# Attention with wider products, masks on GpSimd and another order of the work

## The chip, the cores and the metric

The kernel runs on one core of one Trainium2 chip. The metric is the device time of one execution in microseconds (us); less is better. Some runs are also recorded by the hardware profiler, and all stretches below are us from the start of such a record.

## The reference

Three parts follow each other. Attention runs over 4 batches x 8 heads of 576 rows and 64 columns:

```python
scores = scale * np.matmul(q, k.transpose(0, 1, 3, 2))
scores = np.where(causal, -1000000000.0, scores)
scores = scores - scores.max(-1, keepdims=True)
a = np.exp(scores)
a /= a.sum(-1, keepdims=True) + 1e-09
local = np.matmul(a, v)
...
mem_out = mem_ret / mem_norm
g = 1.0 / (1.0 + np.exp(-beta))[None, :, None, None]
return (g * mem_out + (1 - g) * local).astype(np.float32)
```

`mem_ret` and `mem_norm` are products of phi(q) with a matrix and a vector per head. The 2304 rows of the result then go to 8 experts (each row to one, at most 288 rows to each, chosen by a greedy pass over sorted gate logits), through two layers of the expert, and through a last block `max(x @ w1, x @ w2, x @ w3) @ w_out`.

## The kernel before

Everything is float32, most of it split into a high and a low part that are multiplied separately. The work of attention is a list of tasks in 16 pairs of heads; pair p has keys around 10 p. `Plan.run` (L143) sets the order: it always takes the task that can start first by the costs written beside the tasks (us x 1000), and the lower key among equals. Each engine then executes its own tasks in that order. `PRIO` (L59) holds the offsets of the keys.

For one pair:

- SyncE's queue loads K (`Kr`), Q (`Qr`), Q again for the memory part (`QN`), V, V transposed (`VT`) and the memory matrix (`MZ`) (L316 to L333). ScalarE casts high parts (`KX`, `QX`, `KB`), VectorE subtracts low parts (L353, L358).
- Scores (`piece`, L386): TensorE makes Q x K in blocks of the PSUM tile `s`, each begun by a mask product (`mask_s`, L394, 128 columns), and VectorE takes row maxima from it (`nm`, L413). TensorE turns the maxima (L440), ScalarE copies them (`nmt`) and its own DMA queue writes them as a row of the low part of Q (`QL`, L449 and L450).
- Transposed scores (`score`, `tprod`, L549): the tile `t` holds K x Q less the maxima, from a product with `KX` (L557) and one with `KB` and `QL` (L558). Diagonal blocks begin with a mask product (`mask_t`, L556): five blocks per head, four of 128 columns and one of 64. There are three groups of 512 columns per head and a small one for both. ScalarE takes the exponential into `PT` (L575, L577).
- Output products (`fAV`, L585): for row block j (0 to 4), blocks kb up to j of `PT` are the weights, and 73 columns of V (64 of V, 8 of the expert gate, one of ones) stream. A float32 product is two instructions, so a pair has 60. VectorE divides by the sums and adds the memory part (`norm`, L610). There is one PSUM tile `av` for all pairs.
- Gate products (`g0`, L460): V transposed times 16 columns of the gate matrix `WB`, ten instructions; ScalarE copies them into V (L466). Memory products (`mem`, L509): phi times `MZ`, 146 columns, in two parts. The 16 gate columns of `MZ` are copied by GpSimd (L489) from `MG`, which four groups of small products make at the start from the matrix `mT` (in the tile `m2raw`, L685 to L703).

`fill` (L673) is 48 matmuls of zeros that the first output products wait for; they run where TensorE has nothing else in the start. Between the pairs 24 loads and conversions of the last block's weights are spread (`conv`, L723). Routing and experts follow as a second plan. `ML` (L1074) is the low part of those weights, in 12 tiles.

Of the kernel before, what the change touches and what calls it, by code (L numbers as in the profile page):

```python
# [17 lines left out]
try:  # L18
# [22 lines left out]
FILL = 48  # L41
# [17 lines left out]
PRIO = {"load": -14, "prep": -12, "cb": 3, "S": -11, "N": -11, "nmte": "ACT", "G": -4, "phi": -6, "mem": (-2, -1), "memx": "ACT", "T": 0, "E": 0, "A": 4,  # L59
        "norm": 4, "gate": -9, "m2": (4.0, 6.3, 6.0)}  # L60
# [6 lines left out]
def rows(j):  # L67
    return 128 if j < 4 else 64
# [159 lines left out]
def attention(g, tc, ctx, consts, beta, qT, kT, qN, v1, vT, mz, mT, wg, xd, L, m2):  # L228
# [15 lines left out]
    mt = cs.tile([128, 128], BF, name="mask_t")  # L244
# [4 lines left out]
    G.affine_select(mt, zero[:, :128], pattern=[[1, 128]], compare_op=OP.is_ge, fill=MASK, base=0, channel_multiplier=-1)  # L249
# [13 lines left out]
    WB = cs.tile([128, H // 2, 2, E], F32, name="wb")  # L263
# [4 lines left out]
    def ldw(e):  # L268
        for i in range(2):
            nc.sync.dma_start(WB[64 * i:64 * i + 64, :, i], wg.rearrange("(c i d) e -> i d c e", i=2, d=64)[i])  # L270

# [35 lines left out]
    def pair(p):  # L307
# [30 lines left out]
        for u, (a, z) in enumerate(parts):  # L338
# [35 lines left out]
            tcb.append(add(k + W["cb"], {"ACT": act(w)}, cb, [tK[u], tkb[p] if p < len(KB) else None],  # L374
                           use=U_("Kr") + ([] if not u else U_("KB")), **N_("KB")))
            tsq.append(add(k + W["cb"] + .01, {"DVE": dve(w)}, sq, [tcq[u]], use=U_("Qr", "QX") + ([] if not u else U_("QL")), **N_("QL")))
# [9 lines left out]
        def piece(key, prods, reds):  # L386
# [18 lines left out]
            cost = sum(mm(z - a) * (1 if j < 4 else 2) + 60 * diag for j, i, a, z, c, diag in prods)  # L405
# [13 lines left out]
        for i in range(2):  # L419
            piece(ks + .1 * i, [(3, i, 0, 512, 0, True)], [(0, 512, 1, 4 * i + 3, 0)])  # L420
        for i in range(2):
            piece(ks + .2 + .1 * i, [(2, i, 0, 384, 0, True)], [(0, 384, 1, 4 * i + 2, 0)])
        if p == 0:
            for i in range(2):
                piece(ks + .4 + .1 * i, [(1, i, 0, 256, 0, True), (0, i, 0, 128, 256, True)], [(0, 256, 1, 4 * i + 1, 0), (256, 128, 1, 4 * i, 0)])
            piece(ks + .6, [(4, 2, 512, 576, 0, True)], [(0, 64, 1, 9, 0)])
        else:
            for i in range(2):
                piece(ks + .4 + .1 * i, [(1, i, 0, 256, 0, True), (0, i, 0, 128, 256, True)] + [(4, 2, 512, 576, 384, True)] * i,
                      [(0, 256, 1, 4 * i + 1, 0), (256, 128, 1, 4 * i, 0)] + [(384, 64, 1, 9, 0)] * i)  # L430
        piece(ks + .7, [(4, 2, 0, 512, 0, False)], [(0, 512, 1, 8, 0)])
# [28 lines left out]
        def g0(e):  # L460
            for j in range(NJ):
                PE.matmul(MEM[:rows(j), 4 * C + 16 * j:4 * C + 16 * j + 16], r.VT[:, 128 * j:128 * j + rows(j)],  # L462
                          WB[:, pp].rearrange("p i e -> p (i e)"), start=True, stop=True)

# [84 lines left out]
        def tprod(o, i, gr, c):  # L549
            for kb, a, z in gr:  # L550
# [3 lines left out]
                diag = a == 128 * kb  # L554
                if diag:
                    PE.matmul(o[:kr, c:c + kr], identb[:kr, :kr], mt[:kr, :kr], start=True, stop=False, skip_group_check=True)  # L556
                PE.matmul(d, r.KX[:, i, ks_], r.QX[:, i, a:z], start=not diag, stop=False, skip_group_check=True)  # L557
                PE.matmul(d, r.KB[:, i, ks_], r.QL[:, i, a:z], start=False, stop=True, skip_group_check=True)  # L558
                c += z - a

        def score(key, items, out):
# [9 lines left out]
            def fE(e):  # L571
                if not hasattr(r, "PT"):
                    r.PT = tile("PT", [128, 2, 1600])
                if len(items) > 1:
                    A.activation(r.PT[:64, :, 1536:], o.t[:64, :128].rearrange("p (i q) -> p i q", i=2), AF.Exp, scale=0.125)  # L575
# [18 lines left out]
        outs = []  # L594
# [12 lines left out]
        kq = n + 3 + W["norm"]  # L607
# [80 lines left out]
    for b in range(B):  # L688
        bm = Buf(R["mem"])

        def f0(e, b=b):
            for c in range(4):
                m = mt_.t[:, (4 * b + c) * 64:(4 * b + c) * 64 + 64]
                for i in range(2):
                    PE.matmul(MEM[64 * i:64 * i + 64, 8 * c:8 * c + 8], m, WB[:, c, i], start=True, stop=True)

# [5 lines left out]
        t = add(-10.5, {"PE": 600}, f0, [tl, twb], new=[bm], use=[bt])  # L702
        tmg.append(add(-10.4, {"ACT": 156}, f1, [t], use=[bm]))  # L703
# [739 lines left out]
```

## Time and profile before

| | |
|---|---|
| median of 3 runs | 933.59 us (929.9 to 953.56) |
| the profiled execution | 935.49 us |
| its span, first to last instruction | 933.8 us |
| mean granted TensorE clock | 0.935 of full speed |
| TensorE busy | 889.8 us, 95% of the span |
| VectorE, ScalarE, GpSimd busy | 572.9, 365.2 and 80.0 us |

A row of the profile names the line, the engine, the operation, and the tiles as out<-in. PE is TensorE, DVE is VectorE, ACT is ScalarE, POOL is GpSimd, SPq and ACTq are the DMA queues that SyncE and ScalarE issue. The clock that was granted to TensorE is given as a share of full speed. Matmuls overlap, so from one start to the next is what a product costs, and the length of one is longer than that.

### The profile page before, as it was taken

What the parts mean: (1) busy time and instruction counts of PE and PEld (TensorE: products, weight loads), DVE (VectorE), ACT (ScalarE), POOL (GpSimd) and SP (SyncE); (2) the same over time, 40 slices, a digit from 0 to 9 for tenths busy, and PEclk for the clock granted to TensorE, in tenths of its full rate; (3) what the DMA queues carried; (4) which work ended last, traced back from release to release, by engine and by line L of the source; (5) the groups of instructions that cost most, each with busy time, mean ns of one, the idle gap of its engine ahead of it and who ended that gap; (6) DMA issues with size and microseconds to landing.
All of it is one profiled execution on the core that took longest, in us unless ns stands there. A gap on an engine that the chain in (4) does not pass through costs nothing.

```text
span 933.8 us, 17447 instructions
## 1 busy us (share of the span) xinstructions
PE 889.8 (95%) x6880; PEld 811.5 (87%) x6880; DVE 572.9 (61%) x1481; ACT 365.2 (39%) x826; POOL 80.0 (9%) x145
## 2 busy tenths in 40 slices
PE   7999999999999937989999999999999999999997
PEld 5788888888888827889999999999899999999996
DVE  5456876767567489897577478377277463343421
ACT  3546566566645531322331341331331332432311
POOL 1000000000100005520200200200200201000001
PEclk8578999989889957979999999999999999999999
DMA  7546755465451116142440440530540441230100
GB/s 181 147 113 173 198 166 169 142 185 154 134 194 49 47 61 152 46 90 96 94 136 1 95 135 2 112 118 1 90 151 2 98 131 27 100 104 1 46 1 34
DMA packets 38529, 92.82 MB, mean 99 GB/s; under 512 B 10096, under 2 KB 12272, under 8 KB 38448
## 3 DMA queue, kind: packets, MB, share of 16 engines
q1 hardware_dynamic: 35152, 82.20, 29.3%
q0 software_dynamic: 2976, 9.44, 6.2%
q8 instruction: 54, 0.88, 0.4%
q14 instruction: 27, 0.22, 0.1%
q10 hardware_dynamic: 320, 0.07, 0.0%
HBM read 82.18 MB, written 9.45 MB: 98 GB/s over the span
## 4 chain that ended last, share of the span: by engine, by line
PE 76%; issue 14%; DVE 4%; POOL 1%; DMA 1%; ACT 1%; ACTq 1%; SPq 1%; POOLq 0%; DVEq 0%
PE av L591 12%; PE w L1187 9%; PE w L1189 9%; PE w L1188 9%; PE acc L1188 4%; PE acc L1187 4%; PE acc L1189 4%; PE t L557 4%; PE mem L509 3%; PE t L558 3%; PE s L396 3%; PE rps L935 2%; PE mem L462 1%; PE t L556 1%; PE s L400 1%
## 5 line engine op out<-in xcount | busy, mean ns | idle before, releaser
L1187 PE MATMUL w<-yh,mh 128*128 128x288 f32 x576 | 174.3, 303 | 0.0
L1189 PE MATMUL w<-yh,ml 128*128 128x288 f32 x576 | 170.3, 296 | 0.0
L1188 PE MATMUL w<-yl,mh 128*128 128x288 f32 x576 | 170.1, 295 | 0.0
L591 PE MATMUL av<-V,PT 128*128 128x73 f32 (+2 forms) x960 | 128.4, 286 | 1.6 <-ACT PT L575 0.7
L591 PEld LDWEIGHTS av<-V,PT 128*128 128x128 f32 (+2 forms) x960 | 116.1, 194 | 9.0 <-ACT PT L575 1.5
L1187 PEld LDWEIGHTS w<-yh,mh 128*128 128x128 f32 x576 | 109.2, 190 | 3.0
L1188 PEld LDWEIGHTS w<-yl,mh 128*128 128x128 f32 x576 | 109.0, 189 | 2.9
L1189 PEld LDWEIGHTS w<-yh,ml 128*128 128x128 f32 x576 | 109.0, 189 | 0.0
L1158 DVE TENSOR_TENSOR wlo<-wraw,whi 128x1024 fp32r<-128x1024 f32 x64 | 80.1, 1253 | 41.5 <-ACT whi L1154 41.4
L1292 DVE TENSOR_TENSOR mt<-w,mt 128x288 f32<-128x288 f32 x96 | 43.6, 454 | 80.2 <-PE w L1189 78.0
L577 ACT ACTIVATE PT<-t 128x512 f32<-128x512 f32 x96 | 56.6, 609 | 87.0 <-PE t L558 85.8
L1154 ACT CAST whi<-wraw 128x1024 fp32r<-128x1024 f32 x64 | 66.8, 1049 | 40.3 <-PE acc L1188 22.2
L1188 PE MATMUL acc<-hl,whi 128*128 128x288 f32 x256 | 77.2, 302 | 3.2 <-DVE hl L1095 2.7
L1187 PE MATMUL acc<-hh,whi 128*128 128x288 f32 x256 | 77.0, 301 | 1.0 <-ACT hh L1089 1.0
L413 DVE TENSOR_REDUCE nm<-s 128x1 fp32r<-128x512 f32 (+4 forms) x160 | 69.1, 471 | 13.9 <-PE s L396 11.7
L1189 PE MATMUL w<-xhi,wlo 128*128 128x288 f32 x256 | 76.4, 298 | 1.1 <-DVE wlo L1158 1.1
L1187 PE MATMUL w<-xhi,whi 128*128 128x288 f32 x256 | 76.9, 300 | 0.0
L1188 PE MATMUL w<-xlo,whi 128*128 128x288 f32 x256 | 76.4, 298 | 0.0
L1189 PE MATMUL acc<-hh,wlo 128*128 128x288 f32 x256 | 76.0, 297 | 0.0
L1054 ACT CAST gc<-mt 128x32 fp32r<-128x32 f32 (+2 forms) x72 | 17.5, 243 | 143.4 <-DVE mt L1292 143.4
L557 PE MATMUL t<-QX,KX 128*128 128x512 f32 (+2 forms) x192 | 70.0, 366 | 0.0
L1095 DVE SCALAR_TENSOR_TENSOR hl<-w,hh 128x288 fp32r<-128x288 f32 x64 | 29.0, 455 | 63.3 <-ACT hh L1089 61.3
(222 smaller groups left out, 1821.4 us busy)
## 6 DMA issues: line engine op xcount, KB each, us to landing
wraw<-in_wr SPq DMA_DIRECT2D x64, 512.0 KB
Qr<-in_qT SPq DMA_DIRECT2D x30, 288.0 KB
m2raw<-in_m2w SPq DMA_DIRECT2D x12, 512.0 KB
V<-in_v SPq DMA_DIRECT2D x16, 365.0 KB
QN<-in_qN SPq DMA_DIRECT2D x16, 288.0 KB
VT<-in_vT SPq DMA_DIRECT2D x16, 288.0 KB
Kr<-in_kT SPq DMA_DIRECT2D x15, 288.0 KB
xd<-x SPq DMA_DIRECT2D x16, 256.0 KB
```

The source lines that it names most:

```text
L396: PE.matmul(d, r.QX[:, i, 128 * j:128 * j + 128], r.KX[:, i, a:z], start=False, stop=True, skip_group_check=True)
L413: V.tensor_reduce(r.nm[:, col:col + k], o.s[:, c:c + k * w].rearrange("p (k w) -> p k w", k=k), axis=AX.X, op=OP.max)
L557: PE.matmul(d, r.KX[:, i, ks_], r.QX[:, i, a:z], start=not diag, stop=False, skip_group_check=True)
L577: A.activation(r.PT[:, items[0][0], out:out + 512], o.t, AF.Exp, scale=0.125)
L591: PE.matmul(av[:m, i, j], r.PT[:kr, i, o:o + m], V4()[:kr, kb, i], start=kb == 0, stop=kb == j)
L1095: V.scalar_tensor_tensor(lo(), src(), 0.0, hi().bitcast(F32), op0=OP.max, op1=OP.subtract)
L1154: A.copy(x.W[fb][0], x.RAW[fb])
L1158: V.tensor_sub(x.W[fb][1], x.RAW[fb], x.W[fb][0].bitcast(F32))
L1187: nc.tensor.matmul(o, wh, rh, start=start, stop=False)
L1188: nc.tensor.matmul(o, wh, rl, start=False, stop=False)
L1189: nc.tensor.matmul(o, wl, rh, start=False, stop=stop)
L1292: V.tensor_max(q.mt, o.pt[:, :T], q.mt)
```

## The change

The mask product of the transposed scores goes, and with it the tile `mask_t`; GpSimd sets the masked part of `PT` to zero behind the exponential instead (`select`: two diagonal blocks of a head at once, and the two 64-column blocks together, five per pair). Output products of row blocks 0 to 3 stream 112 columns of V instead of 73, and gate products 112 columns of a gate matrix that is now held three times side by side. The extra columns land in the columns of the next row block, which is written after. The keys change: within a pair, score groups, output blocks and maxima are spread over ten steps, head 1 five steps after head 0; loads are due ten steps earlier; the small products of `mT` get keys 1 to 12; the output tasks' costs are raised. `fill` has 78 matmuls. `ML[0]` gets a tile of its own.

```diff
-FILL = 48
+FILL = 78
...
-PRIO = {"load": -14, "prep": -12, "cb": 3, "S": -11, "N": -11, "nmte": "ACT", "G": -4, "phi": -6, "mem": (-2, -1), "memx": "ACT", "T": 0, "E": 0, "A": 4,
-        "norm": 4, "gate": -9, "m2": (4.0, 6.3, 6.0)}
+PRIO = {"load": -24, "prep": -18, "cb": 8, "S": -14, "ds": 1.2, "N": -5, "nmte": "ACT", "G": -3, "phi": -6, "mem": (1.6, 6.6), "memx": "ACT",
+        "T": (0.5, 2.2, 3.5), "A": 5, "norm": 14, "gate": 6, "m2": (0.0, 6.3, 8.0), "tmg": (1, 6, 9, 12)}
+VW, GW = 112, 112
...
-    G.affine_select(mt, zero[:, :128], pattern=[[1, 128]], compare_op=OP.is_ge, fill=MASK, base=0, channel_multiplier=-1)
...
-    WB = cs.tile([128, H // 2, 2, E], F32, name="wb")
+    WB = cs.tile([128, 3, H // 2, 2, E], F32, name="wb")
...
     def ldw(e):
-        for i in range(2):
-            nc.sync.dma_start(WB[64 * i:64 * i + 64, :, i], wg.rearrange("(c i d) e -> i d c e", i=2, d=64)[i])
+        for a in range(3):
+            for i in range(2):
+                nc.sync.dma_start(WB[64 * i:64 * i + 64, a, :, i], wg.rearrange("(c i d) e -> i d c e", i=2, d=64)[i])
...
         def g0(e):
             for j in range(NJ):
-                PE.matmul(MEM[:rows(j), 4 * C + 16 * j:4 * C + 16 * j + 16], r.VT[:, 128 * j:128 * j + rows(j)],
-                          WB[:, pp].rearrange("p i e -> p (i e)"), start=True, stop=True)
+                w = GW if j < 4 else 16
+                PE.matmul(MEM[:rows(j), 4 * C + 16 * j:4 * C + 16 * j + w], r.VT[:, 128 * j:128 * j + rows(j)],
+                          WB.rearrange("p a c i e -> p (a c i e)")[:, 16 * pp:16 * pp + w], start=True, stop=True)
...
-                diag = a == 128 * kb
-                if diag:
-                    PE.matmul(o[:kr, c:c + kr], identb[:kr, :kr], mt[:kr, :kr], start=True, stop=False, skip_group_check=True)
-                PE.matmul(d, r.KX[:, i, ks_], r.QX[:, i, a:z], start=not diag, stop=False, skip_group_check=True)
-                PE.matmul(d, r.KB[:, i, ks_], r.QL[:, i, a:z], start=False, stop=True, skip_group_check=True)
+                PE.matmul(d, r.KX[:, i, ks_], r.QX[:, i, a:z], start=True, stop=False)
+                PE.matmul(d, r.KB[:, i, ks_], r.QL[:, i, a:z], start=False, stop=True)
...
-                    r.PT = tile("PT", [128, 2, 1600])
+                    r.PT = tile("PT", [128, 2, 1664])
...
-                    PE.matmul(av[:m, i, j], r.PT[:kr, i, o:o + m], V4()[:kr, kb, i], start=kb == 0, stop=kb == j)
+                    c = (2 * kb + i) * C
+                    w = VW if j < 4 else C
+                    PE.matmul(AV[:m, i, j * C:j * C + w], r.PT[:kr, i, o:o + m], r.V[:kr, c:c + w], start=kb == 0, stop=kb == j)
...
+        def select(key, i, kbs, deps):
+            def f(e):
+                m = rows(kbs[0])
+                o = OFFK[kbs[0]]
+                if len(kbs) == 2:
+                    st = OFFK[kbs[1]] - o
+                    v = r.PT[:, i, o:o + 2 * st].rearrange("p (c q) -> p c q", c=2)[:, :, :128]
+                    pat = [[0, 2], [1, m]]
+                else:
+                    v = r.PT[:m, :, o:o + m]
+                    pat = [[0, 2], [1, m]]
+                G.affine_select(v, v, pattern=pat, compare_op=OP.is_ge, fill=0.0, base=0, channel_multiplier=-1)
+            return add(key, {"POOL": 40 + 2.5 * rows(kbs[0])}, f, deps, use=[bf["PT"]])
+
+        outs, mk = [], {}
         for i in range(2):
+            k = n + 5 * i
             for gi, gr in enumerate(groups):
-                ex[i, gi] = score(n + 3 * i + .1 * gi, [(i, gr)], 512 * gi)
-            if i == 1:
-                ex[2, 3] = score(n + 3 * i + .3, [(0, [(4, 512, 576)]), (1, [(4, 512, 576)])], 1536)
+                ex[i, gi] = score(k + W["T"][gi], [(i, gr)], 512 * gi)
+            if i == 0:
+                ex[2, 3] = score(k + W["T"][2] + .1, [(0, [(4, 512, 576)]), (1, [(4, 512, 576)])], 1536)
+                mk[4] = select(k + 4, 0, (4,), [ex[2, 3]])
+            mk[i, 0] = select(k + 2, i, (0, 1), [ex[i, 0], ex[i, 1]])
+            mk[i, 2] = select(k + 4, i, (2, 3), [ex[i, 2]])
...
-                need = [ex[i, x] for x in ((0,), (0, 1), (0, 1, 2), (0, 1, 2), (1, 2))[j]] + [ex[2, 3]] * (j == 4)
-                outs.append(add(n + 3 * i + W["A"] + .1 * j, {"PE": (168, 382, 596, 810, 628)[j]}, fAV(i, j),
+                need = [mk[i, 0]] + [mk[i, 2]] * (j > 1) + [mk[4]] * (j == 4)
+                outs.append(add(n + 5 * i + W["A"] + j, {"PE": (225, 450, 675, 900, 640)[j]}, fAV(i, j),
...
-        t = add(-10.5, {"PE": 600}, f0, [tl, twb], new=[bm], use=[bt])
+        t = add(W["tmg"][b], {"PE": 1000}, f0, [tl, twb], new=[bm], use=[bt])
...
-            ML[k] = wp.tile([128, 1024], F32R, name="ml", tag=f"slot{(k - 1) % 13}")
+            ML[k] = wp.tile([128, 1024], F32R, name="ml", tag=f"slot{k - 1}") if k else mp.tile([128, 1024], F32R, name="ml0")
```

On TensorE, in the middle of attention, this stood from the last transposed scores of a pair on (lines L556 to L558 are transposed scores and their mask, L591 output, L462 gate, L509 memory; a count xN counts products, of which a float32 one is two instructions):

```order
L556 LDWEIGHTS identb
L556 MATMUL t<-mask_t,identb 64x64
L557 MATMUL t<-QX,KX 64x64
L558 MATMUL t<-QL,KB_130 64x64
L591 MATMUL av<-V,PT 128x73 x4
L591 MATMUL av<-V,PT 64x73 x5
L462 MATMUL mem<-wb,VT 128x16 x4
L462 MATMUL mem<-wb,VT 64x16
L591 MATMUL av<-V,PT 128x73 x10
L591 MATMUL av<-V,PT 64x73 x5
L509 MATMUL mem<-MZ,phi 128x146 x3
```

And this stands there now, in a later pair (L555 and L556 are now the transposed scores, L400 and L403 are scores):

```order
L403 MATMUL s<-mask_s,identb 128x64
L555 MATMUL t<-QX,KX 128x64
L556 MATMUL t<-QL,KB_125 128x64
L555 MATMUL t<-QX,KX 128x448
L556 MATMUL t<-QL,KB_125 128x448
L591 MATMUL av<-V,PT 128x112 x4
L400 MATMUL s<-KX,qj_128 128x512 x2
L555 MATMUL t<-QX,KX 128x320
L556 MATMUL t<-QL,KB_125 128x320
L555 MATMUL t<-QX,KX 128x192
L556 MATMUL t<-QL,KB_125 128x192
```

The run of output and gate products is cut: a row block's products now stand between score products of the next head, and no mask stands before a transposed score.

On ScalarE, in the start, the way from the memory of the first pair's Q (`ph`) to the DMAs that write the maxima of pair 0 into `QL` (what a row waits for stands behind it; DMAHW are the slots of the DMA queues) was:

```order
L478 ACTIVATE ph<-ph 128x576 [waits Activation_49]
L290 COPY V<-mem 128x10x8 [waits DMAHW3_49,DVE_49,PE_49]
L85 ACTIVATE c_127<-bt 128x8 [waits DMAHW4_49]
L86 ACTIVATE c_128<-bt 128x8
L290 COPY nmt<-s 9x128 [waits PE_49]
L449 DMA QL<-nmt 1x4x128 [waits DMAHW1_49,Activation_49]
L449 DMA QL<-nmt 1x4x128
L450 DMA QL<-nmt 1x2x64 [waits DMAHW6_49]
```

It is now:

```order
L479 ACTIVATE ph<-ph 128x576 [waits Activation_49]
L290 CAST KX<-Kr 64x1152 [waits DMAHW0_49]
L290 CAST KB_126<-Kr 64x1152
L290 COPY nmt<-s 9x128 [waits PE_49]
L290 CAST QX<-Qr 128x1152 [waits DMAHW2_49,DMAHW1_49]
L290 CAST qj_128<-Qr 128x2x64
L449 DMA QL<-nmt 1x4x128 [waits Activation_49]
L449 DMA QL<-nmt 1x4x128
L450 DMA QL<-nmt 1x2x64 [waits DMAHW4_49]
```

The copies that wait for V and for beta have moved behind the DMAs, and the casts of pair 1 (1152 columns) have moved ahead of them. On SyncE the loads of pair 1 now stand before `mT` and behind six loads of `wb`; before, `mT` stood before them and two loads of `wb` at the front.

On GpSimd, in the pairs, there was nothing but the copies into `MZ`, fourteen in a row. Now it holds:

```order
L605 AFFINE_SELECT PT<-PT 128x2x128 x3
L605 AFFINE_SELECT PT<-PT 64x2x64
L605 AFFINE_SELECT PT<-PT 128x2x128
L290 COPY MZ<-mg 128x2x8
L605 AFFINE_SELECT PT<-PT 128x2x128 x3
```

Five selects and one copy make a pair, and every select stands behind a copy.

## Rows read from the trace of the kernel before

**Rows 1.** The page, the span in 40 equal slices.

```profile
PEclk8578999989889957979999999999999999999999
...
GB/s 181 147 113 173 198 166 169 142 185 154 134 194 49 47 61 152 46 90 96 94 136 1 95 135 2 112 118 1 90 151 2 98 131 27 100 104 1 46 1 34
```

**Rows 2.** The chain that ended last, near the end of attention: start, length, what.

```profile
325.26 2.05 PE av L591 x18
```

**Rows 3.** Busy us by stretch: PE, PEld, DVE, ACT, POOL; clock, DMA share, GB/s.

```profile
16.40:57.40 41.00, 38.53 (x210) 31.62 (x210) 14.67 (x30) 16.40 (x38) 0.63 (x3) 0.50 0.57 144
57.40:327.30 269.90, 268.27 (x1999) 225.51 (x1998) 184.53 (x437) 164.93 (x389) 8.26 (x45) 0.94 0.49 145
80.60:97.60 17.00, 17.00 (x138) 14.48 (x137) 13.22 (x31) 12.16 (x30) 0.21 (x1) 1.00 0.65 174
149.60:169.80 20.20, 20.05 (x138) 17.23 (x137) 12.66 (x31) 11.29 (x26) 0.73 (x1) 0.83 0.52 147
160.00:165.00 5.00, 5.00 (x26) 4.57 (x26) 1.52 (x2) 2.70 (x4) 0.00 (x0) 0.50 0.35 115
97.60:149.60 52.00, 52.00 (x411) 43.11 (x410) 38.84 (x91) 34.21 (x81) 0.96 (x3) 1.00 0.63 185
```

**Rows 4.** Timeline of PE, three runs of equal products at full clock: start, length.

```profile
90.46 2.06 PE L591 MATMUL av<-V,PT 128*128 128x73 f32 x17
...
88.17 0.93 PE L462 MATMUL mem<-wb,VT 128*128 128x16 f32 x7
...
93.71 0.66 PE L509 MATMUL mem<-MZ,phi 128*128 128x146 f32 x4
```

**Rows 5.** Timeline of PE, transposed scores with and without their mask, at full clock.

```profile
87.89 0.21 PE L556 MATMUL t<-mask_t,identb 64*64 64x64 bf16 x1
88.03 0.24 PE L557 MATMUL t<-QX,KX 128*64 128x64 f32 x1
...
95.33 0.23 PE L556 MATMUL t<-mask_t,identb 128*128 128x128 bf16 x1
...
95.69 0.39 PE L558 MATMUL t<-QL,KB 65*128 65x512 f32 x1
95.92 0.19 PE L557 MATMUL t<-QX,KX 128*128 128x64 f32 x1
...
97.32 0.23 PE L556 MATMUL t<-mask_t,identb 128*128 128x128 bf16 x1
...
97.53 0.27 PE L558 MATMUL t<-QL,KB 65*128 65x192 f32 x1
97.64 0.25 PE L591 MATMUL av<-V,PT 128*128 128x73 f32 x1
```

**Rows 6.** Timeline of the start, in brackets idle time before and what ended it.

```profile
4.63 1.31 SPq L270 DMA_DIRECT2D wb<-in_wg  x2
...
15.88 1.81 ACTq L449 DMA_DIRECT2D QL<-nmt  x2
18.76 1.03 PE L695 MATMUL mem<-wb,m2raw 128*64 128x8 f32 x16 [4.34 <-DMA m2raw<-in_mT]
19.97 0.60 ACTq L450 DMA_DIRECT2D QL<-nmt  x1
20.65 0.79 PE L558 MATMUL t<-QL,KB 65*128 65x512 f32 x1
21.06 1.15 ACT L290 CAST KX<-Kr 64x1152 fp32r<-64x1152 f32 x1
```

**Rows 7.** Two lines of GpSimd: ns shortest/median/longest, first and last start, forms.

```profile
L245 POOL TENSOR_SCALAR_AFFINE_SELECT mask_s<-zero x1: 292/292/292, 1.7 to 1.7; 128x128 bf16<-128x128 f32 x1
...
L1077 POOL TENSOR_TENSOR ml<-w,mh x24: 717/748/1732, 358.0 to 400.3; 128x256 fp32r<-128x256 f32 x24
```

**Rows 8.** The page's costliest groups: busy us, mean ns of one, idle before.

```profile
L577 ACT ACTIVATE PT<-t 128x512 f32<-128x512 f32 x96 | 56.6, 609 | 87.0 <-PE t L558 85.8
```

**Rows 9.** GpSimd's waits in attention: us in total, times, longest.

```profile
POOL MZ L290 <- DMA MZ<-in_mz: 164.3, 10, 23.9
```

More of the change, by code (lines that the diff above doesn't have):

```diff
@@ L243, in attention @@
     ms = cs.tile([128, 192], BF, name="mask_s")
-    mt = cs.tile([128, 128], BF, name="mask_t")
     G.affine_select(ms[:, :128], zero[:, :128], pattern=[[-1, 128]], compare_op=OP.is_ge, fill=MASK, base=0, channel_multiplier=1)
@@ L373, in pair @@
             tsk.append(add(k + .02, {"DVE": dve(w)}, sk, [tck[u]], use=U_("Kr", "KX")))
-            tcb.append(add(k + W["cb"], {"ACT": act(w)}, cb, [tK[u], tkb[p] if p < len(KB) else None],
+            tcb.append(add(k + W["cb"] * (p > 1), {"ACT": act(w)}, cb, [tK[u], tkb[p] if p < len(KB) else None],
                            use=U_("Kr") + ([] if not u else U_("KB")), **N_("KB")))
-            tsq.append(add(k + W["cb"] + .01, {"DVE": dve(w)}, sq, [tcq[u]], use=U_("Qr", "QX") + ([] if not u else U_("QL")), **N_("QL")))
+            tsq.append(add(k + W["cb"] * (p > 1) + .01, {"DVE": dve(w)}, sq, [tcq[u]], use=U_("Qr", "QX") + ([] if not u else U_("QL")), **N_("QL")))
         def fj(e):
@@ L403, in fS @@
                             PE.matmul(d, identb, ms[:, 128:], start=False, stop=True)
-            cost = sum(mm(z - a) * (1 if j < 4 else 2) + 60 * diag for j, i, a, z, c, diag in prods)
+            cost = sum(mm(z - a) * (1 if j < 4 else 2) + 125 * diag for j, i, a, z, c, diag in prods)
             hs = {i for j, i, *_ in prods}
@@ L572, in fE @@
                 if not hasattr(r, "PT"):
-                    r.PT = tile("PT", [128, 2, 1600])
+                    r.PT = tile("PT", [128, 2, 1664])
                 if len(items) > 1:
-                    A.activation(r.PT[:64, :, 1536:], o.t[:64, :128].rearrange("p (i q) -> p i q", i=2), AF.Exp, scale=0.125)
+                    A.activation(r.PT[:64, :, 1536:1600], o.t[:64, :128].rearrange("p (i q) -> p i q", i=2), AF.Exp, scale=0.125)
                 else:
                     A.activation(r.PT[:, items[0][0], out:out + 512], o.t, AF.Exp, scale=0.125)
-            cost = sum(2 * mm(z - a) + 60 * (a == 128 * kb) for _, gr in items for kb, a, z in gr)
-            t = add(key + W["T"], {"PE": cost}, fT, tck + tcq + tsk + tcb + tsq + [r.tN], new=[bt],
+            cost = sum(2 * mm(z - a) for _, gr in items for kb, a, z in gr)
+            t = add(key, {"PE": cost}, fT, tck + tcq + tsk + tcb + tsq + [r.tN], new=[bt],
                     use=[bf[x] for x in ("KX", "QX", "KB", "QL")])
-            return add(key + W["E"], {"ACT": act(512 if len(items) == 1 else 128, True)}, fE, [t] + list(ex.values())[:1],
+            return add(key, {"ACT": act(512 if len(items) == 1 else 128, True)}, fE, [t] + list(ex.values())[:1],
                        new=[bf["PT"]] if not ex else [], use=[bt] + ([bf["PT"]] if ex else []))
@@ L606, in pair @@
         h = 2 * pp
-        kq = n + 3 + W["norm"]
+        kq = n + W["norm"]
         last = p == NP - 1
@@ L694, in f0 @@
                 for i in range(2):
-                    PE.matmul(MEM[64 * i:64 * i + 64, 8 * c:8 * c + 8], m, WB[:, c, i], start=True, stop=True)
+                    PE.matmul(MEM[64 * i:64 * i + 64, 8 * c:8 * c + 8], m, WB[:, 0, c, i], start=True, stop=True)
         def f1(e, b=b):
@@ L700, in f1 @@
                 copy(e, MG[r, 4 * b:4 * b + 4, i], MEM[r, :32].rearrange("p (c e) -> p c e", c=4))
-        t = add(-10.5, {"PE": 600}, f0, [tl, twb], new=[bm], use=[bt])
-        tmg.append(add(-10.4, {"ACT": 156}, f1, [t], use=[bm]))
+        t = add(W["tmg"][b], {"PE": 1000}, f0, [tl, twb], new=[bm], use=[bt])
+        tmg.append(add(W["tmg"][b] + .1, {"ACT": 156}, f1, [t], use=[bm]))
     for p in range(NP):
```

13 lines of the change are left out of this document (6 added, 7 removed).

## The prediction

> **What bounds the kernel now.** I read the page first, then the busy time by stretch, then TensorE's timeline inside one pair of heads, then the start. The line of granted clocks in the page [rows 1] shows that the clock is low in the first quarter of the run and again around slice 15, where routing starts; from slice 19 on it is full. So the later part of the kernel, where the change gives one low-part tile (`ml0`) a place of its own and moves no instruction, has nothing to give, and the question is the attention part, which ends with its last product at 325.26 + 2.05 = 327.3 us [rows 2].
>
> In attention TensorE has almost no idle time: 268.3 of 269.9 us busy from 57.4 to 327.3 [rows 3]. What changes from stretch to stretch is its speed. One pair takes 17.0 us for 138 recorded matmuls at clock 1.00, and 20.2 us for the same 138 at clock 0.83 [rows 3]. The levels are 2.4 and 1.2 GHz, so 0.83 over 20.2 us is 2 x 0.17 x 20.2 = 6.9 us at half speed, and these cost 3.2 us: 0.47 us lost per us at half speed. VectorE (38.8 of 52.0 us) and the DMA engines (share 0.63) are below TensorE even in the stretch at full clock [rows 3]. TensorE's work and its clock bound attention, therefore.
>
> Where does the clock fall? At 160 to 165 TensorE is busy 5.00 of 5.00 us and the clock is 0.50 [rows 3]: what went before is a run of output products (`av`), not a pause. In such a run 17 products of 73 columns take 2.06 us; with the length of the last one taken off (0.26 to 0.29 in these three runs), they start (2.06 - 0.275)/16 = 0.112 us apart. Gate products of only 16 columns are (0.93 - 0.26)/6 = 0.112 apart, memory products of 146 columns (0.66 - 0.29)/3 = 0.123 [rows 4]. Sixteen and 73 columns cost the same, so the step there is set by something other than the columns, by all appearances the load of 128 columns of weights that each product has before it; 146 columns just exceed it, at 0.123/146 = 0.84 ns a column. By that rate 16 columns stream for 0.013 of the 0.112 us and 73 for 0.061.
>
> **The masks on TensorE (-19 us).** Each pair loses ten mask matmuls of the transposed scores (eight of 128 columns, two of 64). With its mask the first 512-column product needs 95.69 - 95.33 = 0.36 us until the next starts; the second product of the same width, without a mask, 95.92 - 95.69 = 0.23 [rows 5]: 0.13 saved. For 192 columns it is 97.53 - 97.32 = 0.21 against 97.64 - 97.53 = 0.11: 0.10. The widths between (448, 320) lie between, 0.12 each. That is 0.47 per head, 0.94 per pair. A mask of the 64-column blocks has 88.03 - 87.89 = 0.14 until its product starts, 0.28 for the two, of which I take 0.25 (0.1 to 0.4, as the products beside it may move closer or wait for their own weights). So 1.2 us per pair, 16 x 1.2 = 19 us at full clock (16 to 21), and a pair of 52.0/3 = 17.3 us (three pairs at full clock [rows 3]) becomes 16.1.
>
> **Wider products (0).** Forty output instructions per pair (a float32 product is two) and eight gate instructions go to 112 columns. That lies between 73 columns (0.112 apart) and 146 (0.123) [rows 4]. I take no cost, since at 0.84 ns a column 112 columns stream for 0.094 and still fit under 0.112. The other end: a straight line between the two gives 0.006 more for each, 0.006 x 48 x 16 = 5 us.
>
> **The clock (-15 and -15.7 us).** At 112 columns the array streams for 0.094 of every 0.112 us in the runs after which the clock fell, against 0.061 with 73 columns and 0.013 with 16. The order now also cuts these runs: in a pair, score products stand between the fourth output block and the rest. I expect full clock through the pairs. From 57.4 to 327.3 the mean clock is 0.94 [rows 3]: 2 x 0.06 x 269.9 = 32 us at half speed, times 0.47 = 15 us returned. The first stretch, 16.4 to 57.4, is wholly at 0.50 with 38.5 us busy [rows 3]: 18.1 us lost. The clock will probably still fall once in the start, as TensorE waits there (below); I leave 5 us at half speed, so 33.5 x 0.47 = 15.7 returned. Bounds: nothing at all, or everything (15 + 18).
>
> The row says that the clock fell in a stretch without a pause [rows 3]. The Trainium skill (TensorE: Matmul & The Clock Gate, section Why this matters for your kernels) says that the clock is kept by leaving no idle gaps between bursts of matmuls. By that rule wider products change nothing, and the trace disagrees with it at 160 us: 5.00 of 5.00 busy at 0.50. It stands below as a rival.
>
> **The start (+3 us).** Now the first transposed score waits for the maxima to be written into `QL` by DMA: issued at 15.88 (two) and 19.97, product at 20.65 [rows 6]; the matrix `m2raw` is first used at 18.76 [rows 6]. In ScalarE's new order the casts of pair 1's K and Q (1.15 us each, by the K row [rows 6]) stand ahead of these DMAs, and they wait for loads of pair 1. The K of pair 1 has landed by 19.97 (the third DMA's issue waits for the queue slot of that load), with `m2raw` (512 KB, 2.9 us at the 181 GB/s of that slice [rows 1]) ahead of it. Now `m2raw` comes after, but six small loads of `wb` instead of two: about +1.6 (an estimate: two take 1.31 us to issue [rows 6], and landing may be quicker than that). So K at 18.7; Q (576 KB at the same rate) 3.2 later at 21.9; cast until 23.1, the small cast behind it until 23.4; then the `QL` DMAs, the last issued 1.81 later, and the product 0.68 after that, as now [rows 6]: 25.9, which is 5.3 us later than 20.65. In the wait TensorE does four score pieces and the gate product of pair 1, 1.3 + 1.2 us by the steps seen above, which before came later. Net 2.8, taken as 3 (0 to 8). The 30 more warm-up matmuls lie in the wait, and so do the larger zeroing of `wb` on GpSimd and the matrix products of `tmg`, which move from the front of the queue into the pairs (4 x 1.03 us at half speed now, the same or less then).
>
> **Masks on GpSimd, and new waits (+3 us).** Five selects per pair. One of 128 columns took 0.29 us [rows 7], so 256 columns about 0.5. One subtraction on GpSimd took 0.72 to 1.73 us for the same shape [rows 7]; I read the spread as VectorE's use of SBUF beside it. So a select may take 0.5 to 1.5, five of them 2.5 to 7.5 of the 16.1 us of a pair. An output block waits now for score, exponential (0.61 [rows 8]), select. Between the second score group of a head and its first output block stand some 4.7 us of products in the new order, by the steps seen above [rows 4, 5] (four output blocks 0.9, scores 1.35, five 64-column blocks 0.95, the next head's first group and two pieces 1.2, memory 0.3), and some 3.5 us between the third group and the blocks that need it. That covers 0.61 + 1.5 and the hand-offs, if ScalarE is on time. I take 0.2 us per pair, 3 us (0 to 16). VectorE's and ScalarE's own work is the same, VectorE at 12.9 of 16.1 us.
>
> **The sum.** -19 - 15 - 15.7 + 3 + 3 = -43.7. The profiled execution took 935.5 us (span 933.8): 891.8, so 892. The median of the runs shown, 933.6, is 2 us below the profiled one; the difference is inside the spread.
>
> **Rivals.**
> - The clock does not come back early: ScalarE's and GpSimd's new waits keep the start at half speed for the 41 us of today. Then the 15.7 is not returned: 907. For it: TensorE idles twice in the start. Against: without masks and with wide products every run there streams more. 0.14.
> - Selects are late by 1.2 us per pair more than I allow: 892 + 19 - 3 = 908. For it: 1.73 against 0.72 [rows 7]. 0.13.
> - The clock follows pauses alone (the rule above), and stays low as now. Only the masks count, 22 us with those at half speed: 935.5 - 22 + 6 = 919.5. 0.10.
> - Slower: GpSimd's queue is in order, and between the selects stand the copies into `MZ`, which wait for a load: ten such waits took 164 us in all, up to 23.9 [rows 9], with nothing behind them now. In the new queue four or five selects stand behind each copy. If SyncE issues `MZ` late, the output blocks of a head wait. Above 43.7/16 + 0.2 = 2.9 us of waiting per pair it costs more than all gains; at 4 us per pair the time is 892 + 16 x 3.8 = 953. Against: loads now have a key ten lower (-24 for -14), so they are due earlier. 0.05.
>
> **How the numbers follow.** The forecast has 0.58. Its own range is 882 to 902 (start 0 to 8, waits 0 to 8). The range given reaches over the first two rivals, 880 to 916, and leaves out the third and the fourth and the far tails, near 0.2. Two per cent of 933.6 (about what a measurement of this kernel can tell from no change) is 18.7, so faster means below 914.9: 0.85. The third rival is within: 0.10. Slower: 0.05.
>
> **What would show it.** Right: clock 1.00 in every stretch from about 30 us to the end of attention; a pair of 16.1 us; output products 0.112 apart at 112 columns; attention ending near 284; the rest as long as before. Wrong: output products 0.13 apart or more; TensorE idle before output blocks with a select as releaser; stretches at 0.50 in the pairs; a first transposed score after 30 us.

## The result, and the profile after

The changed kernel takes 893.4 us (median of 4 runs, 891.1 to 896.4); the kernel before took 934.5 us beside it (930 to 954). The ratio is 0.958, 95% interval 0.952 to 0.964. A later series gave 895.2 us (6 runs) and a ratio of 0.962 (0.955 to 0.969). The forecast was 892, range 880 to 916. Runs of one kernel differ by how long the clock stood at half speed, so the ratios compare the runs near each kernel's fastest; the table further down has all runs.

The page of the changed kernel, granted clock in 40 slices:

```profile
PEclk9999999999999579799999999999999999999999
```

The low first quarter of [rows 1] is gone. What is left is the dip of routing, which comes earlier now.

The changed kernel by stretch (columns as in [rows 3]: length, busy us of PE, PEld, DVE, ACT, POOL, then clock, DMA share, GB/s):

```profile
22.00:33.00 11.00, 9.18 (x88) 7.66 (x88) 5.05 (x12) 6.75 (x17) 2.34 (x6) 1.00 0.92 222
33.00:36.40 3.40, 3.40 (x17) 3.17 (x16) 1.28 (x5) 1.34 (x6) 0.29 (x1) 0.50 0.42 91
36.40:286.10 249.70, 242.36 (x1932) 211.84 (x1930) 194.83 (x448) 170.55 (x402) 43.41 (x122) 1.00 0.57 162
...
286.10:371.20 85.10, 60.05 (x604) 56.58 (x605) 74.30 (x227) 23.69 (x34) 31.19 (x29) 0.74 0.32 90
371.20:894.40 523.20, 512.82 (x3990) 490.50 (x3989) 286.81 (x757) 153.91 (x353) 37.44 (x56) 1.00 0.27 71
...
67.20:263.10 195.90, 191.60 (x1514) 167.90 (x1514) 162.22 (x371) 136.08 (x318) 34.80 (x104) 1.00 0.63 182
```

The kernel before, the same two stretches behind attention:

```profile
327.30:412.40 85.10, 59.80 (x602) 56.32 (x603) 74.14 (x227) 23.75 (x34) 30.84 (x29) 0.74 0.32 90
412.40:933.70 521.30, 511.30 (x3992) 489.01 (x3991) 286.93 (x757) 154.11 (x353) 37.59 (x56) 1.00 0.27 71
```

Everything behind attention takes as long as before: routing 85.10 us in both, the rest 523.2 for 521.3. The chain of the changed kernel ends attention here (start, length, what; compare [rows 2]):

```profile
283.30 2.75 PE av L591 x24
```

That is 286.1 for 327.3: the 41.2 us were all won in attention. There the clock fell once in this profile, for the 3.4 us from 33.0 on, and was full up to the end. A second profile of the same kernel (e11 below) has one drop more, of 3.4 us from 48.7 on, behind a pause of TensorE (timeline and stretch):

```profile
47.66 0.64 PE L713 MATMUL mem<-wb,m2raw 128*64 128x8 f32 x16 [0.95 <-ACT x L533]
...
48.80:52.10 3.30, 3.30 (x14) 2.48 (x13) 1.21 (x2) 1.34 (x3) 0.67 (x1) 0.50 0.67 208
```

The last row of the stretches above runs from the first output product of the third pair to that of the fifteenth: 195.9/12 = 16.3 us for a pair, against 17.0 to 17.3 at full clock and 20.2 with a drop before [rows 3].

The timeline of TensorE in the changed kernel (start, length, what, in brackets idle time before and what ended it):

```profile
22.18 0.40 PE L555 MATMUL t<-QX,KX 128*128 128x512 f32 x1
22.41 0.40 PE L556 MATMUL t<-QL,KB 65*128 65x512 f32 x1
...
28.23 0.64 PE L713 MATMUL mem<-wb,m2raw 128*64 128x8 f32 x16 [0.47 <-ACT mg L290]
...
31.77 0.50 PE L396 MATMUL s<-KX,QX 128*128 128x512 f32 x1 [1.33 <-ACT QX L290]
...
105.69 1.36 PE L463 MATMUL mem<-wb,VT 128*128 128x112 f32 x10
...
115.59 2.38 PE L591 MATMUL av<-V,PT 128*128 128x112 f32 x20
```

With the last one's 0.28 taken off, output products of 112 columns start (2.38 - 0.28)/19 = 0.111 us apart, gate products (1.36 - 0.28)/9 = 0.120; with 73 and 16 columns both took 0.112 [rows 4]. The first transposed score starts at 22.2 to 22.4, not at the 25.9 that I had worked out. ScalarE's timeline shows how the DMAs into `QL` got out earlier:

```profile
14.90 1.15 ACT L290 CAST KX<-Kr 64x1152 fp32r<-64x1152 f32 x1 [5.52 <-DMA Kr<-in_kT]
...
17.50 1.15 ACT L290 CAST QX<-Qr 128x1152 fp32r<-128x1152 f32 x1 [0.23 <-DMA Qr<-in_qT]
...
19.40 0.60 ACTq L450 DMA_DIRECT2D QL<-nmt  x1
```

Pair 1's K had landed by 14.9 and its Q by 17.5, where I had put them at 18.7 and 21.9; the last DMA into `QL` was issued at 19.4. SyncE's queue issued the six loads of `wb` and then that K so:

```profile
6.76 3.96 SPq L270 DMA_DIRECT2D wb<-in_wg  x6
10.76 0.61 SPq L323 DMA_DIRECT2D Kr<-in_kT  x1
```

The waits of the changed kernel from 16 to 286 us (us in total, times, longest), and its selects (ns shortest/median/longest):

```profile
POOL PT L605 <- ACT PT L575: 221.8, 62, 21.5
...
POOL MZ L290 <- DMA MZ<-in_mz: 5.6, 2, 3.5
PE mem L463 <- ACT x L533: 3.8, 7, 1.0
```

```profile
L605 POOL TENSOR_SCALAR_AFFINE_SELECT PT<-PT x80: 285/409/1522, 25.3 to 278.9; 128x256 f32<-128x256 f32 x64, 64x128 f32<-64x128 f32 x16
```

GpSimd waits for exponentials most of the time, its copies into `MZ` hardly ever wait for their load any more ([rows 9]: 164 us), and no wait of TensorE names a select. The one new wait of some size is that of gate products for ScalarE's reading of the tile `mem`, 3.8 us.

### The profile page after: what moved, and what is told of

Read it like the earlier page. It is cut to its first block, busy times and chain, and to the rows that moved or that the text cites. A ratio compares the mean times of both kernels' runs of the same rounds, so it can differ in the third digit from the quotient of the medians.

```text
span 894.5 us, 17317 instructions
## 1 busy us (share of the span) xinstructions
PE 845.5 (95%) x6750; PEld 783.6 (88%) x6750; DVE 579.0 (65%) x1481; ACT 365.5 (41%) x826; POOL 117.6 (13%) x224
## 4 chain that ended last, share of the span: by engine, by line
PE 63%; issue 16%; DVE 7%; ACT 5%; DMA 4%; ACTq 2%; POOL 1%; SPq 1%; POOLq 0%; DVEq 0%
PE w L1205 9%; PE w L1207 9%; PE w L1206 9%; PE av L591 7%; PE acc L1206 5%; PE acc L1205 4%; PE acc L1207 4%; PE t L555 2%; PE mem L463 2%; PE t L556 2%; PE rps L953 2%; ACT x L533 2%; PE s L396 2%; PE mem L510 2%; DMA Qr<-in_qT 1%
## 5 line engine op out<-in xcount | busy, mean ns | idle before, releaser
L591 PE MATMUL av<-V,PT 128*128 128x112 f32 (+2 forms) x960 | 119.1, 264 | 1.3 <-DVE tmp L642 1.1
L591 PEld LDWEIGHTS av<-V,PT 128*128 128x128 f32 (+2 forms) x960 | 107.5, 174 | 9.0 <-issue 1.0
L1310 DVE TENSOR_TENSOR mt<-w,mt 128x288 f32<-128x288 f32 x96 | 43.7, 455 | 80.5 <-PE w L1207 78.2
L413 DVE TENSOR_REDUCE nm<-s 128x1 fp32r<-128x512 f32 (+4 forms) x160 | 72.4, 475 | 15.5 <-PE s L396 7.0
L1072 ACT CAST gc<-mt 128x32 fp32r<-128x32 f32 (+2 forms) x72 | 17.5, 243 | 143.4 <-DVE mt L1310 143.4
L575 ACT ACTIVATE PT<-t 128x512 f32<-128x512 f32 x96 | 57.7, 602 | 43.7 <-PE t L556 26.9
L1139 POOL DMA_INDIRECT xg<-xd,tidx x24 | 23.8, 991 | 371.0 <-PE w L1207 182.2
```

Of the source, the lines that this page charges most:

```text
L413: V.tensor_reduce(r.nm[:, col:col + k], o.s[:, c:c + k * w].rearrange("p (k w) -> p k w", k=k), axis=AX.X, op=OP.max)
L575: A.activation(r.PT[:, items[0][0], out:out + 512], o.t, AF.Exp, scale=0.125)
L591: PE.matmul(AV[:m, i, j * C:j * C + w], r.PT[:kr, i, o:o + m], r.V[:kr, c:c + w], start=kb == 0, stop=kb == j)
L1139: g.gather = G.indirect_dma_start(out=x.xg[:96, c], out_offset=None, in_=xd, in_offset=bass.IndirectOffsetOnAxis(ap=r.tidx[:96, c:c + 1], ...
L1310: V.tensor_max(q.mt, o.pt[:, :T], q.mt)
```

## Experiments

Eleven more kernels were run, and the changed one again (e11). For every run the time at half speed follows from its mean clock: 2 x (1 - clock) x span, so 2 x 0.029 x 894.5 = 52 us for the profiled run of the changed kernel, routing included. Over the 88 runs for which the clock is on record (29 of the kernel before, 59 of the others, e12 with them) a fit of one slope for all kernels and one constant for each gives

time = time at full clock + 0.434 x (us at half speed), with 1.7 us left over (root mean square). Without e5, whose runs lie farthest out, the slope is 0.420.

So each kernel has two numbers, one for the work and one for the clock:

| kernel | masks | output / gate columns | order | median us (range) | us at half speed, mean (range) | at full clock |
|---|---|---|---|---|---|---|
| before | TensorE | 73 / 16 | old | 937.4 (922.6 to 967.1) | 122 (87 to 187) | 885 |
| e4 | TensorE | 112 / 112 | old | 916.2 (913.9 to 917.9) | 57 (49 to 64) | 891 |
| e10 | TensorE | 73 / 112 | old | 915.5 (913.4 to 928.2) | 76 (62 to 98) | 886 |
| e9 | GpSimd | 73 / 16 | old | 910.2 (902.4 to 920.3) | 96 (74 to 123) | 869 |
| e8 | GpSimd | 112 / 112 | old | 899.4 (897.0 to 903.3) | 66 (61 to 78) | 871 |
| e5 | TensorE | 73 / 16 | new | 990.0 (975.4 to 1057.6) | 274 (206 to 393) | 885 |
| e2 | TensorE | 112 / 112 | new | 907.9 (903.3 to 914.5) | 50 (36 to 68) | 887 |
| e1 | GpSimd | 73 / 16 | new | 944.4 (920.2 to 954.4) | 162 (114 to 192) | 871 |
| e6 | GpSimd | 73 / 112 | new | 899.0 (896.0 to 903.1) | 62 (55 to 70) | 872 |
| e7 | GpSimd | 112 / 16 | new | 901.6 (898.6 to 903.5) | 68 (57 to 76) | 872 |
| changed (and e11) | GpSimd | 112 / 112 | new | 895.1 (891.1 to 901.1) | 47 (36 to 63) | 875 |
| e3 | none | 112 / 112 | new | 896.7 (894.8 to 898.8) | 53 (46 to 63) | 874 |

"New order" is all of the change that is neither mask nor width: keys, loads, warm-up, start. A constant of the fit is good to some 2 us.

### e1: narrow products in the changed kernel

```diff
-VW, GW = 112, 112
+VW, GW = 73, 16
```

> The changed kernel with output and gate products back at 73 and 16 columns (VW, GW = 73, 16), everything else as changed, so the order of every instruction is the same. Theory (the columns keep the clock): in the runs of output and gate products the clock falls to 0.50 again, as before the change; between 15 us (the pairs alone) and 31 us (pairs and start) come back, so 908 to 924 us, and stretches at 0.50 appear in the pairs. Rival (the order that cuts the runs, and the masks gone, keep the clock; the width does nothing): 893 us within 5, clock 1.00 in the pairs and a pair still 16.0 us.

944.4 us, half speed 114 us or more in every run. Two stretches of its profile, a pair at full clock and two later pairs:

```profile
89.60:105.20 15.60, 15.60 (x127) 13.87 (x127) 13.01 (x32) 11.45 (x27) 2.11 (x6) 1.00 0.69 192
...
199.50:254.30 54.80, 54.80 (x244) 48.12 (x244) 25.10 (x56) 22.08 (x51) 8.14 (x43) 0.50 0.36 100
```

TensorE is busy for all of the 54.8 us and stays at 0.50. With not an instruction moved, the columns make the difference; order and missing masks do not keep the clock. The fastest run, 920.2 us, lies within the theory's range; the other three, 941.6 to 954.4, lie above it, with 164 to 192 us at half speed.

### e4: wide products in the kernel before

```diff
+VW, GW = 112, 112
...
-    WB = cs.tile([128, H // 2, 2, E], F32, name="wb")
+    WB = cs.tile([128, 3, H // 2, 2, E], F32, name="wb")
```

with the products of L462 and L591 as in the change.

> The kernel before with only the widths changed: output and gate products stream 112 columns, the gate matrix three times side by side (six small loads); masks on TensorE and the old order stay. Theory (the columns keep the clock, the order does not matter for it): the 15 us of the pairs and up to 15.7 of the start come back, 904 to 919 us, clock 1.00 in the pairs, a pair of 17.2 us. Rival (the clock follows pauses, or the old order's runs of output products bring it down whatever they stream): 934 us within 5, clock 0.50 after those runs as before.

916.2 us, ratio 0.984 (0.975 to 0.993). From the third pair's first output product to the fifteenth's:

```profile
70.60:279.30 208.70, 208.36 (x1635) 173.25 (x1635) 154.75 (x363) 134.94 (x318) 8.30 (x44) 1.00 0.58 168
```

The clock is 1.00 in the pairs in the old order too: 208.7/12 = 17.4 us each. The clock returns about 65 us of half speed, 28 us; 6 of it go to the work at full clock. The start was not freed: it has 20.5 us at half speed in this profile, with pauses.

```profile
15.40:35.90 20.50, 16.26 (x110) 11.73 (x110) 5.17 (x10) 7.56 (x20) 0.45 (x2) 0.50 0.67 163
```

### e6 and e7: one width at a time

```diff
-VW, GW = 112, 112
+VW, GW = 73, 112
```

and, for e7, `VW, GW = 112, 16`.

> The changed kernel with output products back at 73 columns, gate products left at 112. Theory (output products, 40 of the 48 widened instructions of a pair, decide the clock): half speed as with both narrow, 114 us or more, 921 us or more. Rival (the run of gate products, 16 columns at 0.112 us, is the emptiest and decides): clock 1.00 in the pairs, 893 to 897 us.

> The changed kernel with gate products back at 16 columns, output products left at 112. Theory (eight gate instructions a pair, about 0.9 us of 16, between products that stream, do not bring the clock down): 891 to 897 us, clock 1.00 in the pairs. Rival (the emptiest run decides): half-speed stretches in the pairs, 905 us or more.

899.0 and 901.6 us: either width alone brings most of what both bring. e6's theory falls, and its rival is right on the clock, at 2 us more than it gave: wide gate products are enough in the pairs. With them alone wide (e6) the profile has no drop in the pairs; the third to fifteenth pair:

```profile
66.90:262.60 195.70, 190.98 (x1513) 167.09 (x1512) 162.02 (x371) 136.05 (x318) 34.44 (x104) 1.00 0.62 182
```

That is also 195.7 us against 195.9 with both wide, so widening output products costs nothing here. With narrow gate products (e7) the clock fell four times in the pairs, for 3.4 to 6.8 us, and the mean is 0.96:

```profile
57.40:297.30 239.90, 233.20 (x1782) 205.12 (x1782) 182.86 (x419) 157.88 (x369) 41.31 (x117) 0.96 0.54 159
```

There too the rival is right in kind, at a smaller price (901.6 for its 905). So the 16-column products alone can bring the clock down, but wide output products help too: with both narrow (e1) every run was at least 16 us longer than any of e7.

### e10: wide gate products alone, in the kernel before

The diff is e4's without the change of L591.

> The kernel before with only the gate products at 112 columns (gate matrix three times side by side); output products at 73, masks on TensorE, old order. Theory (the emptiest run of a pair is the gate run amid output products, and filling it is enough): clock 1.00 in nearly all pairs, 912 to 922 us, as with both wide. Rival (one width is enough only in the new order, which cuts the runs): half-speed stretches in every second pair as before, 928 to 942 us.

915.5 us, ratio 0.982 (0.970 to 0.994), as much as with both widths. The third to fifteenth pair:

```profile
79.30:286.20 206.90, 206.55 (x1635) 172.56 (x1633) 154.67 (x362) 134.71 (x318) 9.46 (x44) 1.00 0.58 170
```

With only eight of a pair's 48 instructions widened the clock is 1.00 in the pairs of this profile, at 206.9/12 = 17.2 us a pair, 0.15 less than with wide output products (e4). Only the start is as low as before (44 us at half speed in this profile).

### e2 and e3: masks back on TensorE, and no masks

```diff
...
+                if diag:
+                    PE.matmul(o[:kr, c:c + kr], identb[:kr, :kr], mt[:kr, :kr], start=True, stop=False, skip_group_check=True)
...
-                G.affine_select(v, v, pattern=pat, compare_op=OP.is_ge, fill=0.0, base=0, channel_multiplier=-1)
+                return
```

for e2; e3 has the last two lines alone.

> The changed kernel with the mask product of the transposed scores back on TensorE and nothing done on GpSimd in its place; planned order as changed. Theory (ten mask products are 1.2 us of TensorE in each pair): 893 + 16 x 1.2 = 912 us (909 to 914), a pair of 17.2 us, clock still 1.00 in the pairs. Rival (what the masks cost on TensorE, the selects cost in waits): 893 to 898 us.

> The changed kernel with the five selects of each pair left out, so that the masked probabilities stay in the sums; nothing takes their place. Theory (the selects lie beside other work and cost at most 0.2 us a pair): 890 to 893 us. Rival (output products wait for selects): 893 less 0.5 to 1 us a pair, 877 to 885 us.

907.9 and 896.7 us. The third to fifteenth pair of e2, and a stretch of its start:

```profile
75.10:281.90 206.80, 205.85 (x1634) 174.88 (x1633) 160.35 (x370) 138.13 (x318) 6.00 (x44) 1.00 0.61 174
...
21.60:42.10 20.50, 20.50 (x110) 17.02 (x109) 6.82 (x18) 6.73 (x17) 1.17 (x2) 0.50 0.60 143
```

and of e3:

```profile
67.00:262.20 195.20, 191.44 (x1513) 167.91 (x1512) 159.90 (x370) 136.21 (x318) 7.98 (x44) 1.00 0.64 182
```

At full clock a pair is 17.2 us with masks on TensorE, 16.3 with selects, 16.3 with neither. The masks cost (206.8 - 195.2)/12 = 0.97 us a pair, 15.5 in 16 pairs, and the selects 0.06, 1 us in all. Both theories are right in kind, and both times missed their ranges: e2 came out below 909 to 914, as the masks cost 0.97 for 1.2, and e3 above 890 to 893. In e2's profile the start also stayed at half speed for 20.5 us, TensorE busy throughout; that run took 914.5 us, the other three 903 to 909. (e3 itself ran no faster than the changed kernel: 896.7 against 893.4 and 895.2.)

### e9 and e8: selects in the old order

The masks leave TensorE and `select` stands behind the exponentials, with keys `n + 3 * i + .15` and `.25` (and `.35` for the small one); the planned cost of a score product loses its mask, so the order is planned anew by the old keys. e8 has the widths of 112 as well.

> The kernel before with the masks as selects on GpSimd and nothing else: narrow products, old order. Theory (in the old order the dense score products stand together and bring the clock back soon after it fell; what made it stay low with narrow products was the new order, not the missing masks): half-speed stretches of 10 us or less in the pairs, 80 to 130 us at half speed in all, 874 + 0.42 x 80 to 130 = 908 to 929 us. Rival (with the masks gone too few columns stream, and the clock stays low in any order): 150 us or more at half speed, 937 us or more.

> The kernel before with the widths of 112 and the masks as selects on GpSimd, in the old order: only the new order, its start and its warm-up are missing. Theory (masks are worth 13 us of full-clock time in either order, the order 4): the kernel before with wide products alone took 916 us, less 13 gives 903 us (899 to 907), few waits of output products for selects. Rival (the old order has output products close behind their scores, so selects are late there, 0.5 us a pair or more, and the new order is what hides them): 911 us or more, with TensorE waiting for selects before output products.

910.2 us for e9, half speed 74 to 123 us. Two stretches of its profile:

```profile
150.00:163.00 13.00, 11.46 (x92) 10.03 (x91) 10.51 (x25) 10.64 (x26) 4.96 (x6) 1.00 0.43 117
163.00:169.50 6.50, 6.50 (x31) 5.37 (x31) 2.13 (x6) 0.00 (x0) 0.00 (x0) 0.50 0.68 222
```

In this profile a drop in the pairs lasts 6.8 or 10.2 us and ends. The theory holds: in the old order the clock does not stay low without masks, narrow products or not. e8 took 899.4 us, and TensorE's waits for selects were, in e8:

```profile
PE av L590 <- POOL PT L604: 1.3, 3, 0.9
```

1.3 us in the whole of attention. The theory had 903 (899 to 907), and the rival, late selects in the old order, falls; the new order was not needed to hide them. But in e8's profile the clock fell even with both widths at 112: in the start, and for 10.2 us in the pairs, a little behind a pause of 1.12 us:

```profile
18.90:36.00 17.10, 12.87 (x91) 9.98 (x92) 4.88 (x8) 7.12 (x16) 1.21 (x4) 0.50 0.65 147
...
67.98 0.30 PE L555 MATMUL t<-QL,KB 65*128 65x64 f32 x1 [1.12 <-DMA QL<-nmt]
...
70.20:80.30 10.10, 10.10 (x44) 8.64 (x44) 5.98 (x14) 7.78 (x21) 2.27 (x4) 0.50 0.29 70
```

### e5: the new order alone

Both diffs of e1 and e2 together.

> The changed kernel with narrow products (73 and 16 columns) and the mask products of the transposed scores on TensorE, nothing on GpSimd: of the change only the new order, the start and the warm-up are left. The runs so far fit time = full-clock time + 0.42 us per us at half speed, with 887 for the kernel before and 873 for the changed one with narrow products, which spent 114 to 192 us at half speed. Theory (mask products are streamed columns too, and keep the clock a little where the output products don't): full-clock time 887, half speed less than with the masks gone, 80 to 120 us, so 920 to 938 us. Rival (the new order itself brings the clock down): half speed 114 to 192 us as with the masks gone, 935 to 967 us.

990.0 us (975.4 to 1057.6), over 50 slower than the kernel before by the medians, past what either side expected. Five pairs early, two stretches within them, and four pairs late:

```profile
87.30:172.90 85.60, 85.60 (x676) 73.19 (x676) 67.76 (x157) 58.48 (x133) 0.99 (x5) 0.98 0.65 186
...
120.10:130.10 10.00, 10.00 (x87) 9.06 (x87) 8.51 (x17) 7.38 (x14) 0.20 (x1) 1.00 0.74 216
130.20:133.50 3.30, 3.30 (x16) 3.22 (x14) 2.51 (x9) 0.94 (x4) 0.00 (x0) 0.50 0.88 224
...
216.40:339.30 122.90, 122.90 (x546) 104.71 (x545) 54.09 (x123) 45.64 (x103) 4.20 (x36) 0.50 0.26 81
```

A pair goes from 17.1 to 30.7 us. The clock fell at 130.2 behind 10 us without any pause, and was back after 3.4 us. It fell again at 201.8 and did not come back for the rest of attention, though TensorE is busy for all of the 122.9 us. The rival had the direction right: with narrow products the new order is harmful.

### e11 and e12: the changed kernel again, and two small edits

```diff
-WARM2 = 140
+WARM2 = 200
...
-"G": -3
+"G": -1
```

> The changed kernel once more, as the reference for the next kernel on the same chip: 889 to 897 us.

> The changed kernel with two small edits: the key of the gate products two steps later (G -1 for -3), so that they no longer follow the second memory part whose tile ScalarE still reads, and 200 warm-up products for 140 (WARM2) ahead of the first expert. Theory: the 3.8 us in which gate products wait for ScalarE go, and the half-speed stretch of 6.8 us at the first expert, worth 0.42 x 6.8 = 2.8 us: 887 us (885 to 890). Rival (the gate product's wait moves to the memory part, or the warm-up holds up routing by 60 x 0.054 = 3.2 us): 891 to 896 us.

895.2 us (893.0 to 901.1) and 893.4 us (892.4 to 896.0), 6 runs each: no difference that these runs can tell, and e12 within its rival's 891 to 896. In e12 the wait of gate products for ScalarE went from 3.4 us (in e11) to 2.7, and the half-speed stretch at the first expert did not go but came later, in two parts of 3.4 us (at 333.0 and 346.7). Both edits missed what they were meant for; whether one of the rival's two reasons holds was not looked into.

## Why the prediction was right, point by point

**The sum.** Predicted: 43.7 less. Beside each other the two kernels have medians 41 us apart, and the ratio 0.958 stands for 39 us. Means of all runs are 938.2 before and 895.0 changed, 43.2 less; of these the table gives 885 - 875 = 11 (before rounding) to work at full clock and 75 us less at half speed x 0.434 = 32 to the clock. The forecast had 13 and 30.7. That the sum came so close is partly luck: the gain from the masks was put too high, and so were the costs of the selects and of the start, and these errors cancel. And the lower end 882 does not follow from the two ranges named beside it: 892 - 3 - 3 is 886.

**Masks and selects (-19 + 3).** Right in sum, each mis-sized. The four pairs of kernels that differ in this alone give, at full clock, -16 (e9 less before), -20 (e8 less e4), -14 (e1 less e5) and -12 (changed less e2), on average -16, which is what the two terms add up to. Each was too large by itself: the masks are 0.97 a pair, not 1.2, and the selects cost 1 us, not 3. The products beside a mask move closer when it goes, so its 0.13 from one start to the next is not all won; that this is the reason was not tried by itself.

**Wider products (0, bound +5).** Mis-sized by a little: the four pairs of kernels give +6, +2, +2 and +4 at full clock. The pairs show +0.15 us each from output products in the old order (e4 against e10) and nothing in the new one (e6). The price rule held for output products, 0.111 apart; gate products went to 0.120, 0.008 x 8 x 16 = 1 us.

**The clock (-30.7).** Right in sum, -32. Right in mechanism: e1, e4 and e10 change the columns and not the order, and the long stretches at half speed in the pairs come and go with them. The price of half speed was 0.434, not 0.47. The 5 us left at half speed in the start were 3.4, behind the pauses of 0.47 and 1.33 us at 28 to 32 us. Three parts of the reasoning were wrong. I counted on the output products, 40 of 48 instructions; eight gate instructions did it alone (e10). "The order now also cuts these runs" spoke as if that helped: alone it costs over 50 us (e5), and with wide products it is worth 7 to 19 us at half speed (e4 to e2, e8 to changed). And I put the 15.7 us of the start down to columns and masks; with both in the old order the profile (e8) still has 17 us at half speed there, so some of the gain came with the new order.

**The rule on pauses (rival, 0.10).** It falls as the only cause. The changed kernel pauses for 249.7 - 242.4 = 7.3 us from 36.4 on at clock 1.00; the kernel before pauses for 1.6 us [rows 3] and has 0.94. In e4 the pauses of the stretch shown are 208.7 - 208.4 = 0.3 us, and the time is 916 us instead of 937. Four of the five drops in the pairs before follow waits of 0.15 to 0.19 us that e4 and e10 do not have, the one at 159.8 this wait:

```profile
158.91 5.87 PE L591 MATMUL av<-V,PT 64*64 64x73 f32 x32 [0.15 <-ACT PT L575]
```

But the drop at 130.2 in e5 follows 10.00 of 10.00 us busy. Pauses may have a part where products are wide: the drops at 33.0 (changed), 48.7 (e11) and 70.1 (e8) each come 1 to 2 us behind one of 0.95 to 1.33 us. The Trainium skill (TensorE: Matmul & The Clock Gate, section Why this matters for your kernels) asks for no idle gaps; these three drops point its way, though the pauses are short, and e5, where 122.9 of 122.9 us are busy at 0.50, disagrees.

**The start (+3).** Mis-sized: the step that failed is the landing of pair 1's loads, 18.7 and 21.9 predicted, 14.9 and 17.5 measured. The 1.6 us for the additional loads of `wb` was not the error: all six took 3.96 us to issue, against 1.31 for two before, and pair 1's K was issued 1.8 us later than before. But it had landed about 4.1 us after its issue. What was too small is the 2.9 us that I took off for `m2raw` no longer standing ahead of it, or else 19.97, by which K was there at the latest, was too late a start; no run separates the two. Old against new order at full clock is -1, -4, +1 and +3 over the four pairs of kernels: 0 on average.

**The other rivals.** Late selects: 1 us. GpSimd's queue held up by `MZ` loads: two waits, 5.6 us, and no wait of TensorE names a select. The clock not coming back early: full from 36.4 on in the one profile, from 52.1 on in the other.

**What stays open.** Why half speed lasts in the new order with narrow products. In the old order the wide score products stand together, and a drop in the pairs ends within 6.8 or 10.2 us (e9); in the new one they alternate with narrow output products and it lasts up to 208 us (e5). But in e5 three drops before that one ended within 6.8 us, and in e1 one lasted 92 us and two others ended within 10.2 us. That the mixing is the cause fits the long ones, but no run changed the mixing alone, and what makes one drop long and another short in the same order is open. Open too is what about the columns counts; that the array stands empty behind the loading of weights was reasoned, not measured.

## What to carry to other kernels

Read the granted clock by stretch before anything else, and price it: here a us at half speed cost 0.43 us, in all of these kernels. Where it falls although TensorE is busy, look for the products that stream the fewest columns per start; they could be padded here at little cost, because their spacing was 0.112 us for 16 and 73 columns and 0.111 to 0.120 for 112, and the few emptiest ones brought most of it. Judge an order of the work only together with the clock that it leads to: by the medians the same order was worth 4 to 8 us with wide products, and cost 34 (e9 to e1) and 53 (before to e5) with narrow ones.

## What the runs showed of the hardware that was not expected

- Half speed can last: 208 us at 0.50 in e5 (from 201.8, the last 30 in routing), with TensorE 122.9 of 122.9 us busy in the stretch shown.
- The clock can fall without a pause: at 130.2 in e5, behind 10.00 us busy of 10.00.
- Time is linear in the us at half speed, with one slope (0.434) for kernels from 891 to 1058 us.
- Widening eight gate instructions a pair from 16 to 112 columns (1 us in 17) took the drops out of the pairs (e10: clock 0.94 to 1.00 there, 937 to 916 us).
- A select on GpSimd (64 of 80 have 256 columns) takes 0.41 us in the median and up to 1.52.
